# One of the first loads moved to ScalarE's queue, one batch's slots moved behind four value products, and two more clock fillers

## The chip, the cores and the metric

The kernel runs on one core of a Trainium2 chip. The metric is device time of one execution in microseconds, taken as the median of three runs. The engines are called as the profile calls them: PE is TensorE's matrix multiply and PEld its weight load, DVE is VectorE, ACT ScalarE, POOL GpSimd, and SP SyncE, which here issues DMA transfers. The 16 DMA engines of the core carry out what any queue issues.

## The reference

Eight batches of eight heads, 576 positions of 64 numbers, 32 memory slots. A softmax of `phi` over the positions pools `k` and `v` into slots; `q` attends to the slots; the result goes through a gated convolution and two projections.

```python
a = np.exp(phi - phi.max(axis=2)); a = a / (a.sum(axis=2) + 1e-09)
k_m = einsum('bhsm,bhsd->bhmd', a, k);  v_m = einsum('bhsm,bhsd->bhmd', a, v)
scores = q @ k_m.T / sqrt(64);          attn = softmax(scores)
x = (attn @ v_m)                        # heads side by side: 576 x 512 for each batch
gate_pre = sum of conv_w[k] * x shifted by 4 - k positions, k = 0..4
out = (sigmoid(gate_pre) * (x @ w_val)) @ w_out
```

## The kernel before

The program is a list of steps, each a small function of a batch and of a half or a chunk. The string `ORDER` names every step once, and the kernel runs through it from first to last; each step issues its instructions on its engines at that point. So the place of a name in `ORDER` fixes the order of the instructions on every engine, and of the transfers on a DMA queue. An engine takes its instructions strictly in that order. Batches are counted from 0, so the fourth batch has number 3. A star behind a step's name makes it take its other engine.

The steps that matter here:

- `load_top.0.g` brings `phi` of the first batch, group g of four heads, laid out along the positions; `phi_max`, `phi_open` (an exponential on ACT), `phi_turn` (PE transposes) and `phi_place` (a copy, on ACT for group 1 and with a star on DVE for group 0) turn it into the weights `e`.
- `load_kv.0.g.x` brings `k` with a column of ones (x = 1) or `v` (x = 0) of the first batch's group g. `kv_77` is group 0's tile in the listings below, `kv_78` group 1's. All loads are issued by SP.
- `slots.0.g.1` multiplies `e` of group g with its `k` (40 matmul rows of the profile for each g); group 1's last chunk reads `kv_77`. `slots_inv`, `slots_scale` and `slots_turn` divide by the sum and transpose, `slots_place` copies into `kvT`; `scores.0.0` needs `kvT` and the half of `q` that `load_q.0.0` brings.
- `warm.n` is a filler: a product of the identity with n copies of itself, 128 x 128n, which nothing reads. `spread_taps` prepares the convolution's weights on PE.
- In a later batch `slots.b` takes both groups, k and v at once (80 matmul rows of 128x129). `conv.b.s` is the convolution of half s on PE, `value.b.s.t` a quarter of the values' product, which `gated.b.s.y` (DVE) multiplies with the gate two quarters at a time, `project.c` the last projection of a chunk, `mix.b.s` the attention's values.

PSUM has eight banks. `Banks.take` gives a step the banks that were given back longest ago, and a step waits until the one that held them before has read them. DMA completions are counted on eight semaphores that are dealt out in the order of issue.

Of the kernel before, what the change touches and what calls it, by code (L numbers as in the profile page):

```python
# [59 lines left out]
soft_top.0.0 phi_max.1 warm.4 soft_exp.0.0 load_kv.0.1.0 phi_open.1.0 warm.4 spread_taps.0 scores.0.1 place_taps.0  # L60
phi_open.1.1 narrow_sign.o.0 phi_turn.1.0 soft_norm.0.0 narrow_add.o.0 scores_turn.0.1 load_w.v.2 phi_place.1.0
load_w.v.0 soft_top.0.1* load_w.o.1 load_w.v.3 load_rest.1 load_w.p.0 soft_turn.0.0 load_w.o.2 slots.0.0.0 slots.0.1.0
slots_scale.0.0* soft_exp.0.1 phi_turn.1.1 taps.0.0* taps.0.1* wo_high.0* slots_turn.0.0 narrow_round.v.2 load_kv.1.0
conv.0.0 phi_place.1.1 narrow_round.v.0 narrow_size.v.0 soft_high.0.0* narrow_sign.v.0 soft_norm.0.1* slots_place.0.0*
val_rows.0.1 load_kv.1.1 soft_low.0.0 narrow_size.v.2 narrow_add.v.0 soft_turn.0.1 gate.0.0.1 gate.0.0.0 val_rows.0.0
narrow_round.v.3 val_high.0.0* narrow_round.p.0 val_high.0.1* narrow_sign.v.2 narrow_size.v.3 soft_high.0.1*
narrow_sign.v.3 load_top.2 val_low.0.0 conv.0.1 wo_low.0 narrow_size.o.2 value.0.0.0 val_low.0.1 soft_low.0.1
narrow_add.v.2 narrow_add.v.3 value.0.1.0 value.0.0.1 gate.0.1.1 narrow_round.o.2 narrow_sign.p.0 narrow_size.p.0
load_q.1 gate.0.1.0 value.0.1.1 narrow_sign.o.2 narrow_size.o.1 val_rows.0.3 val_rows.0.2 gated.0.0.0 val_high.0.3
val_high.0.2 gated_high.0.0.0 narrow_round.o.1 narrow_sign.o.1 val_low.0.2 val_low.0.3 gated.0.1.0 slots.1 slots_inv.1  # L70
slots_scale.1 value.0.1.2 narrow_add.o.2 phi_max.2 wo_high.2 taps.1.0* gated_low.0.0.0 value.0.0.2 slots_turn.1
value.0.0.3 gated.0.0.1 load_w.o.3 value.0.1.3 gated_high.0.1.0 load_rest.2 narrow_add.o.1 narrow_add.p.0 wo_high.1
gated.0.1.1 wo_low.1 slots_place.1 scores.1.0 wo_low.2 gated_low.0.1.0 scores.1.1 val_rows.1 project.0.0
scores_turn.1.0 project.3.0 phi_spread.2 scores_turn.1.1 narrow_size.o.3 narrow_round.o.3 soft_top.1* narrow_sign.o.3
gated_high.0.0.1 narrow_add.o.3 val_high.1 wo_high.3 project.2.0 load_phi.2 project.1.0 gated_low.0.0.1 soft_exp.1
wo_low.3 load_kv.2.0 val_low.1 gated_high.0.1.1 soft_norm.1* project.0.1 project.1.1 phi_shift.2 soft_turn.1.0
taps.1.1 place.0 gated_low.0.1.1 load_top.3 load_kv.2.1 phi_max.3 soft_turn.1.1 phi_exp.2 mix.1.0 soft_high.1*
scaled.1.0.3.0 scaled.1.0.3.3 tap.1.0.0.0 tap.1.0.1.0 scaled.1.0.2.0 slots.2 tap.1.0.0.4 slots_inv.2 soft_low.1
place.1 scaled.1.0.2.4 tap.1.0.1.2 tap.1.0.0.1 tap.1.0.1.4 slots_scale.2* tap.1.0.0.2 scaled.1.0.3.4 tap.1.0.1.1
# [10 lines left out]
store.1 gated_low.1.1.0* add.2.0.1.1 project.5.1 tap.2.0.0.1 tap.2.0.1.4 scaled.2.0.3.2 scaled.2.0.2.2 place.4  # L90
load_phi.4 load_kv.4.1 add.2.0.1.3 add.2.0.1.2 store.4 tap.2.0.1.2 soft_high.2 soft_low.2 place.5 scores.3.0
tap.2.0.0.3 scores.3.1 val_rows.2 scores_turn.3.0 scores_turn.3.1 mix.2.1 add.2.0.1.4 val_high.2 soft_top.3 load_phi.5
scaled.2.1.2.2 scaled.2.1.3.2 project.6.0 val_low.2 tap.2.1.0.0 scaled.2.1.2.0 tap.2.1.1.0 store.5 phi_max.5
project.7.0 store.2 tap.2.1.1.3 scaled.2.1.2.4 open_gate.2.0.1 tap.2.1.0.3 scaled.2.1.3.1 load_top.6 scaled.2.1.3.4
value.2.0.2 scaled.2.1.3.0 value.2.0.3 scaled.2.1.2.1 add.2.1.1.1 soft_exp.3 tap.2.1.1.2 tap.2.1.0.4 gated.2.0.1
project.6.1 tap.2.1.0.2 project.7.1 add.2.1.1.4 place.6 tap.2.1.0.1 tap.2.1.1.1 value.2.0.0 scaled.2.1.3.3
scaled.2.1.2.3 soft_norm.3 tap.2.1.1.4 value.2.0.1 phi_spread.4 project.8.0 value.2.1.0 project.8.1 gated_high.2.0.1
place.7 open_gate.2.0.0 gated_low.2.0.1 gated.2.0.0 value.2.1.1 gated_high.2.0.0 phi_shift.4* soft_turn.3.0
soft_turn.3.1 open_gate.2.1.0 phi_exp.4 load_q.4 store.6 val_rows.3 add.2.1.1.3 gated_low.2.0.0 soft_high.3
gated.2.1.0 val_high.3 phi_max.6 mix.3.0 tap.3.0.0.0 scaled.3.0.2.0 place.8* scaled.3.0.3.3 slots.4 tap.3.0.1.0  # L100
scaled.3.0.3.0 project.9.0 val_low.3 tap.3.0.0.1 add.2.1.1.2 value.2.1.2 tap.3.0.1.1 tap.3.0.0.4 slots_inv.4
tap.3.0.1.2 scaled.3.0.2.3 add.3.0.1.3 value.2.1.3 scaled.3.0.2.1 scaled.3.0.3.1 scaled.3.0.2.4 gated_high.2.1.0
soft_low.3 open_gate.2.1.1 load_top.7 scaled.3.0.3.4 scaled.3.0.2.2 project.9.1 tap.3.0.0.3 gated.2.1.1 slots_scale.4
scaled.3.0.3.2 tap.3.0.0.2 tap.3.0.1.3 tap.3.0.1.4 mix.3.1 project.10.0 place.9 tap.3.1.1.0 add.3.0.1.4 add.3.0.1.2
tap.3.1.1.1 value.3.0.0 value.3.0.1 tap.3.1.1.3 tap.3.1.1.4 tap.3.1.1.2 tap.3.1.0.0 store.7 open_gate.3.0.0
gated.3.0.0 project.10.1 slots_turn.4 add.3.0.1.1 scaled.3.1.3.0 gated_low.2.1.0 value.3.0.2 scaled.3.1.2.2
gated_high.2.1.1 value.3.0.3 scaled.3.1.2.0 scaled.3.1.3.2 tap.3.1.0.4 scaled.3.1.3.3 scaled.3.1.3.4 place.10
slots_place.4 open_gate.3.0.1 gated_low.2.1.1 tap.3.1.0.1 scores.4.0 add.3.1.1.2 tap.3.1.0.2 tap.3.1.0.3 scores.4.1
gated.3.0.1 val_rows.4 load_kv.5.1 store.9 load_kv.5.0 scores_turn.4.0 load_rest.6 scores_turn.4.1 phi_spread.5
load_q.5 scaled.3.1.2.3 project.12.0 project.11.0 soft_top.4* store.10 gated_high.3.0.0 phi_shift.5 scaled.3.1.3.1  # L110
val_high.4 gated_low.3.0.0 scaled.3.1.2.4 scaled.3.1.2.1 project.11.1 val_low.4 soft_exp.4 soft_norm.4* value.3.1.0
value.3.1.1 project.12.1 add.3.1.1.4 add.3.1.1.3 phi_exp.5 gated_high.3.0.1 open_gate.3.1.0 value.3.1.2 add.3.1.1.1
place.11 place.12 value.3.1.3 soft_turn.4.0 gated.3.1.0 open_gate.3.1.1 mix.4.0 tap.4.0.1.0 tap.4.0.0.0 scaled.4.0.3.1
# [711 lines left out]
```

## Time and profile before

| | us |
|---|---|
| median of three runs (236.61 to 239.53) | 237.48 |
| the profiled execution | 237.75 |
| its span in the profile | 236.0 |
| PE busy | 226.2 |
| DVE, ACT, POOL busy | 185.4, 169.4, 170.2 |

The profiled execution lies 0.27 above the median, and 1.75 of its time lies around the span. PE is busy 96% of the span, so what matters is where it isn't, and which of these gaps other work sets.

### The profile page before, as it was taken

Reading aid. Unit: us, or ns where it says so; the run is one execution under the profiler, and the core shown is the slowest. Engines: PE = TensorE matmul, PEld = TensorE weight load, DVE = VectorE, ACT = ScalarE, POOL = GpSimd, SP = SyncE. Lnnn points to the kernel's source line nnn. Section 1 sums busy time; section 2 is a strip of 40 time slices with the busy share of each in tenths; the row PEclk is TensorE's granted clock in tenths of the full one; section 3 lists DMA queues with packets and bytes.
Section 4 is the critical chain, followed back from the end, with each engine's and each line's share of the span. In section 5 each row is a group of like instructions: output and inputs, shape, how many; then the busy total and the mean of one; then the engine's idle time right before and its main releaser. Section 6 shows DMA issues by size and latency. Waiting matters only on the chain.

```text
span 236.0 us, 6170 instructions
## 1 busy us (share of the span) xinstructions
PE 226.2 (96%) x2496; PEld 175.1 (74%) x2496; DVE 185.4 (79%) x304; ACT 169.4 (72%) x338; POOL 170.2 (72%) x132
## 2 busy tenths in 40 slices
...
GB/s 190 372 413 404 416 410 385 416 207 335 364 138 287 420 287 219 99 274 227 247 157 37 327 375 350 259 0 111 267 7 44 87 49 46 44 92 44 44 64 159
DMA packets 14653, 51.17 MB, mean 217 GB/s; under 512 B 1658, under 2 KB 1954, under 8 KB 11938
## 3 DMA queue, kind: packets, MB, share of 16 engines
...
q8 instruction: 19, 0.31, 0.6%
q14 instruction: 8, 0.07, 0.1%
...
## 4 chain that ended last, share of the span: by engine, by line
PE 90%; DMA 4%; ACT 2%; SPq 1%; issue 1%; POOL 1%
PE banks L727 43%; PE banks L692 22%; PE banks L467 8%; PE banks L626 6%; PE banks L514 4%; DMA q<-in_first_dram 4%; PE banks L593 3%; PE banks L280 1%; PE banks L436 1%; PE banks L498 1%; POOL w_val_sb L381 1%; PE banks L388 1%; ACT o L367 0%; SPq L308 0%; SPq L341 0%
## 5 line engine op out<-in xcount | busy, mean ns | idle before, releaser
L670 POOL TENSOR_TENSOR gate<-gate,x 128x576 f32<-128x576 f32 x49 | 71.7, 1464 | 15.4 <-ACT gate L662 5.3
L727 PE MATMUL banks<-woH,hL 128*128 128x512 f32 x144 | 58.2, 404 | 0.0
L727 PE MATMUL banks<-woH,hH 128*128 128x512 f32 x144 | 56.4, 392 | 0.0
L727 PE MATMUL banks<-woL,hH 128*128 128x512 f32 x144 | 56.3, 391 | 0.0
L662 ACT ACTIVATE x<-banks,cwP 128x288 f32<-128x288 f32 x104 | 48.6, 529 | 5.7 <-PE banks L626 3.7
L653 DVE SCALAR_TENSOR_TENSOR gate<-banks,cwP,gate 128x288 f32<-128x288 f32 x104 | 49.1, 508 | 2.1 <-ACT gate L651 1.2
L267 POOL TENSOR_TENSOR hL<-h,hH 128x576 fp32r<-128x576 f32 (+8 forms) x38 | 38.0, 1019 | 7.8 <-DVE hH L264 4.5
L698 DVE SCALAR_TENSOR_TENSOR h<-gate,banks 128x576 f32<-128x576 f32 x32 | 23.9, 749 | 16.5 <-PE banks L692 12.5
L727 PEld LDWEIGHTS banks<-woH,hL 128*128 128x128 f32 x144 | 27.0, 188 | 9.3 <-issue 2.1
L727 PEld LDWEIGHTS banks<-woH,hH 128*128 128x128 f32 x144 | 27.0, 188 | 6.0
L741 ACT ACTIVATE o<-banks 128x512 f32<-128x512 f32 x26 | 15.7, 603 | 21.1 <-PE banks L727 19.6
L727 PEld LDWEIGHTS banks<-woL,hH 128*128 128x128 f32 x144 | 27.1, 188 | 4.6
L692 PE MATMUL banks<-pL,vwH 128*128 128x288 f32 x128 | 28.6, 305 | 0.0
L692 PE MATMUL banks<-pH,vwH 128*128 128x288 f32 x128 | 27.3, 294 | 0.0
L692 PE MATMUL banks<-pH,vwL 128*128 128x288 f32 x128 | 27.3, 294 | 0.0
L692 PEld LDWEIGHTS banks<-pL,vwH 128*128 128x128 f32 x128 | 21.2, 188 | 6.1 <-issue 3.6
L264 ACT CAST hH<-h 128x576 fp32r<-128x576 f32 (+8 forms) x38 | 18.8, 531 | 7.3 <-DVE h L698 7.3
L267 POOL TENSOR_TENSOR pL<-pT,pH 128x1152 fp32r<-128x1152 f32 (+1 forms) x8 | 19.0, 2372 | 6.4 <-DVE pH L264 6.4
L467 PE MATMUL banks<-kv,e 128*32 128x129 f32 (+2 forms) x656 | 19.3, 263 | 2.8 <-issue 1.4
L675 ACT ACTIVATE gate<-gate 128x576 f32<-128x576 f32 x26 | 18.1, 699 | 4.0 <-DVE gate L653 2.8
L467 PEld LDWEIGHTS banks<-kv,e 128*32 128x32 f32 x656 | 16.3, 128 | 5.7 <-issue 5.3
L692 PEld LDWEIGHTS banks<-pH,vwL 128*128 128x128 f32 x128 | 20.5, 188 | 0.0
...
## 6 DMA issues: line engine op xcount, KB each, us to landing
...
raw<-in_w_val_dram SPq DMA_DIRECT2D x4, 512.0 KB, 10.9
...
```

What stands on the lines that cost most here:

```text
L264: eng.copy(out=out, in_=x) if eng is nc.scalar else eng.tensor_copy(out=out, in_=x)
L267: eng.tensor_tensor(out=out, in0=x, in1=hi.bitcast(F32), op=ALU.subtract)
L467: nc.tensor.matmul(km[j * M:(j + 1) * M, i, n], lhsT=e[:, i, j * M:(j + 1) * M, c], rhs=kvx[c][:, j, :], start=(c == 0), stop=(c == C - 1))
L626: nc.tensor.matmul(live["cv", b, s, g][x * D:(x + 1) * D, t, 0:n], lhsT=weights(g)[rows], rhs=pTs[b % 2][rows, g, s * HALF + i:s * HALF + ...
L653: nc.vector.scalar_tensor_tensor(out=gt, in0=v, scalar=w, in1=gt, op0=ALU.mult, op1=ALU.add)
L662: nc.scalar.activation(out=live[n][:, x], in_=live["cv", b, s, g][:, x, i:i + HALF], func=AF.Identity, scale=cwP[:, 0, i * NP + t:i * NP + ...
L670: eng.tensor_tensor(out=gt, in0=gt, in1=live["x", b, s, g, i], op=ALU.add)
L675: nc.scalar.activation(out=gt, in_=gt, func=AF.Tanh, scale=0.5)
L692: nc.tensor.matmul(vp[:, x, 0:HALF], lhsT=a[:, g, t * P:(t + 1) * P], rhs=p[:, g, s * HALF:(s + 1) * HALF], start=(i == 0), stop=(i == len ...
L698: nc.vector.scalar_tensor_tensor(out=h, in0=live["gate", b, s, y], scalar=1.0, in1=live["vp", b, s, y][:, :, 0:HALF], op0=ALU.add, op1=ALU ...
L727: nc.tensor.matmul(live["proj", c][:, 0], lhsT=ring[a][:, t, at:at + P], rhs=w[:, t], start=(y == 0 and i == 0), stop=(y == 1 and i == len ...
L741: nc.scalar.activation(out=o, in_=x, func=AF.Copy, scale=0.5)
```

## The change

`load_kv.0.1.1`, the `k` of the first batch's group 1, becomes the first step of all, and ACT issues it in place of SP. A `warm.2` stands behind each of the two steps `slots.0.0.1` and `slots.0.1.1`. In the fourth batch `slots.3` and `slots_inv.3` move behind the four steps `value.1.1.2`, `value.1.1.3`, `value.1.0.2` and `value.1.0.3`, with `slots_inv.3` then behind `gated.1.0.1`, and `slots_scale.3*` behind `gated_high.1.1.1`. Nothing else in `ORDER` differs.

```diff
 ORDER = """
-warm.4 warm.4 load_top.0.0 load_w.c.0 load_top.0.1 phi_max.0.0 narrow_size.c.0 phi_open.0.0 phi_max.0.1 phi_open.0.1
...
-load_kv.0.1.1 slots.0.0.1 load_w.v.1 narrow_size.v.1 slots.0.1.1 narrow_add.c.0 load_q.0.0 slots_inv.0.1
...
+load_kv.0.1.1 warm.4 warm.4 load_top.0.0 load_w.c.0 load_top.0.1 phi_max.0.0 narrow_size.c.0 phi_open.0.0 phi_max.0.1
...
+phi_place.0.0* slots.0.0.1 warm.2 load_w.v.1 narrow_size.v.1 slots.0.1.1 warm.2 narrow_add.c.0 load_q.0.0
...
-conv.1.1 slots.3 gate.1.1.1 gated_high.1.0.0 soft_norm.2 value.1.1.2 gate.1.1.0 phi_max.4 slots_inv.3 open_gate.1.0.1
-value.1.1.3 gated.1.1.1 soft_turn.2.0 slots_scale.3* value.1.0.2 load_q.3 value.1.0.3 gated.1.0.1 gated_low.1.0.0
-value.1.1.0 mix.2.0 gated_high.1.1.1 scaled.2.0.2.1 scaled.2.0.2.4 scaled.2.0.3.0 gated_low.1.1.1* value.1.1.1
...
+phi_exp.3 soft_exp.2 add.1.0.1.3 conv.1.1 gate.1.1.1 gated_high.1.0.0 soft_norm.2 value.1.1.2 gate.1.1.0 phi_max.4
+open_gate.1.0.1 value.1.1.3 gated.1.1.1 soft_turn.2.0 value.1.0.2 load_q.3 value.1.0.3 slots.3 gated.1.0.1 slots_inv.3
+gated_low.1.0.0 value.1.1.0 mix.2.0 gated_high.1.1.1 slots_scale.3* scaled.2.0.2.1 scaled.2.0.2.4 scaled.2.0.3.0
...
-        nc.sync.dma_start(out=t, in_=kv[(b - 1) * G + g] if b else piece("vk"[x] + str(g)))
+        rows = kv[(b - 1) * G + g] if b else piece("vk"[x] + str(g))
+        (nc.scalar if (b, g, x) == (0, 1, 1) else nc.sync).dma_start(out=t, in_=rows)
```

The extra line of code moves all line numbers behind it by one in the changed kernel.

On PE at the very start (first batch: fillers, `phi_turn`, `slots`, `spread_taps`, `slots_turn`, `scores`) there stood before:

```order
L422 MATMUL banks<-ident,phT 128x128 x5
L280 MATMUL banks<-ident 128x256
L467 MATMUL banks<-kv_77,e 32x65 x20
L467 MATMUL banks<-kv_78,e 32x65 x16
L467 MATMUL banks<-kv_77,e 32x65 x4
L388 MATMUL banks<-cw_sb,pick_head 128x64 x5
L498 MATMUL banks<-ident,kvd 128x128
L514 MATMUL banks<-q,kvT 32x288 x8
```

and now:

```order
L423 MATMUL banks<-ident,phT 128x128 x5
L280 MATMUL banks<-ident 128x256
L468 MATMUL banks<-kv_77,e 32x65 x20
L280 MATMUL banks<-ident 128x256
L468 MATMUL banks<-kv_78,e 32x65 x16
L468 MATMUL banks<-kv_77,e 32x65 x4
L280 MATMUL banks<-ident 128x256
L389 MATMUL banks<-cw_sb,pick_head 128x64 x5
L499 MATMUL banks<-ident,kvd 128x128
L515 MATMUL banks<-q,kvT 32x288 x8
```

A filler of 128x256 follows each group's products; the order of the rest is kept. On ACT, the first rows of the program (a load of its function table, then the first piece of work on a weight) become

```order
L309 DMA kv_78<-in_first_dram 128x1040
L362 ACT_TABLE_LOAD
L362 ACTIVATE x<-st 40x64
L414 ACTIVATE phT<-phT,top 128x576 x2
L368 ACTIVATE o<-st 40x64
```

where the transfer is the only new row; on SP it is gone from its fifth place, and `w_val`, `q` and `w_out` follow `kv_77` directly. On PE around the fourth batch's slots (behind `conv.1.1`, the row with `taps`) there stood before:

```order
L626 MATMUL banks<-pT_75,taps 64x288 x40
L467 MATMUL banks<-kv_77,e 32x129 x16
L467 MATMUL banks<-rest,e 32x129 x4
L467 MATMUL banks<-kv_78,e 32x129 x16
L467 MATMUL banks<-rest,e 32x129 x4
L692 MATMUL banks<-pL,vwH 128x288 x2
L692 MATMUL banks<-pH,vwL 128x288 x2
L692 MATMUL banks<-pH,vwH 128x288 x2
```

and the end of the same stretch now reads, with four such triples of `value` ahead of it:

```order
L693 MATMUL banks<-pH,vwH 128x288 x2
L468 MATMUL banks<-kv_77,e 32x129 x16
L468 MATMUL banks<-rest,e 32x129 x4
L468 MATMUL banks<-kv_78,e 32x129 x16
L468 MATMUL banks<-rest,e 32x129 x4
L693 MATMUL banks<-pL,vwH 128x288 x2
L693 MATMUL banks<-pH,vwL 128x288 x2
L693 MATMUL banks<-pH,vwH 128x288 x2
L627 MATMUL banks<-pT_73,kvd 64x292 x8
```

The slots now stand one `value` step ahead of `mix.2.0` (the row with `kvd`), instead of directly behind the convolution.

## Rows read from the trace of the kernel before

**Rows 1.** The page: busy time of each engine, share of the span, instructions.

```profile
PE 226.2 (96%) x2496; PEld 175.1 (74%) x2496; DVE 185.4 (79%) x304; ACT 169.4 (72%) x338; POOL 170.2 (72%) x132
```

**Rows 2.** Windows, PE alone: stretch, its length, busy time (rows), granted clock, DMA.

```profile
27.00:64.40 37.40, 37.40 (x641) 1.00 0.92 361
64.46:65.90 1.44, 0.00 (x1) 1.00 0.14 51
67.00:232.40 165.40, 165.40 (x1494) 1.00 0.47 166
```

**Rows 3.** Timeline of the start: start, length, engine, line, what, wait before.

```profile
3.76 0.75 DVE L408 TENSOR_REDUCE top<-phT 128x1 f32<-128x576 f32 x1 [3.76 <-DMA phT<-in_first_dram]
...
5.32 0.75 DVE L408 TENSOR_REDUCE top<-phT 128x1 f32<-128x576 f32 x1 [0.80 <-DMA phT<-in_first_dram]
...
7.62 0.60 PE L280 MATMUL banks<-ident 128*128 128x256 f32 x2
7.83 0.69 ACT L264 COPY e<-banks 128x640 f32<-128x640 f32 x1 [0.63 <-PE banks L422]
...
8.34 0.78 PE L467 MATMUL banks<-kv,e 128*32 128x65 f32 x40
...
9.20 1.04 SPq L308 DMA_DIRECT2D kv<-in_first_dram  x2
...
10.37 0.77 PE L467 MATMUL banks<-kv,e 128*32 128x65 f32 x40 [1.25 <-DMA kv<-in_first_dram]
...
11.07 1.32 PE L388 MATMUL banks<-cw_sb,pick_head 40*128 40x64 f32 x10
...
12.33 0.33 PE L498 MATMUL banks<-ident,kvd 128*128 128x128 f32 x1
12.69 0.29 DVE L264 COPY kvT<-banks 128x128 f32<-128x128 f32 x1 [0.81 <-PE banks L498]
...
13.29 1.22 PE L514 MATMUL banks<-q,kvT 64*32 64x288 f32 x16 [0.64 <-DMA q<-in_first_dram]
...
18.49 0.72 PE L514 MATMUL banks<-q,kvT 64*32 64x288 f32 x16
```

**Rows 4.** Windows of the start: stretch, PE, PEld, DVE, ACT, POOL, clock, DMA share, GB/s.

```profile
1.50:5.30 3.80, 3.76 (x4) 1.15 (x4) 0.75 (x1) 1.53 (x3) 0.00 (x0) 1.00 0.81 245
12.84:16.25 3.41, 2.96 (x18) 1.09 (x19) 1.70 (x4) 2.46 (x5) 1.28 (x1) 0.50 1.04 420
```

**Rows 5.** The four loads of the first batch's k and v, from issue to landing.

```profile
DMA to landing us min/median/max: 6.2/8.7/10.4
```

**Rows 6.** The chain of waits, start: the load of q, the second slots, `val_rows`.

```profile
3.45 9.70 DMA q<-in_first_dram
...
19.99 1.30 PE banks L467 x80
...
26.95 0.45 PE banks L593 x16
```

**Rows 7.** The chain of waits, third batch's slots and around the fourth's.

```profile
51.23 2.37 PE banks L467 x80
...
62.54 1.92 PE banks L467 x61
64.46 1.44 issue
65.90 0.88 PE banks L467 x19
66.78 4.17 PE banks L692 x30
```

**Rows 8.** DMA queues: packets, MB, share; whole span, then only 63.5 to 64.7.

```profile
q8 instruction: 19, 0.31, 0.6%
...
q8 instruction: 1, 0.02, 5.4%
```

**Rows 9.** Timelines of DVE and POOL, 60 to 70.

```profile
62.06 0.75 DVE L698 SCALAR_TENSOR_TENSOR h<-gate,banks 128x576 f32<-128x576 f32 x1
...
65.54 2.13 POOL L559 TENSOR_TENSOR st<-st,ss 128x1152 f32<-128x1152 f32 x1 [1.42 <-DVE ss L558]
```

More of the change, by code (lines that the diff above doesn't have):

```diff
@@ L60 @@
[L60 to L79, printed above, removed]
@@ L90 @@
[L90 to L109, printed above, removed]
@@ L110 @@
[L110 to L113, printed above, removed]
-scaled.4.0.2.3 scaled.4.0.3.0 gated_high.3.1.0* scaled.4.0.2.0 gated.3.1.1 tap.4.0.0.1 phi_spread.6 slots.5
@@ L125 @@
-store.14 phi_spread.7 value.4.0.1 slots.6 value.4.1.0 value.4.1.2 soft_exp.5 phi_shift.7* slots_inv.6 slots_scale.6
-slots_turn.6 phi_exp.7 project.17.0 gated.4.0.0 gated_high.4.0.0 soft_norm.5* open_gate.4.1.0 open_gate.4.1.1
-gated_low.4.0.0 value.4.1.3 value.4.1.1 project.17.1 value.4.0.2 gated.4.1.0 value.4.0.3 slots_place.6 scores.6.0
-gated_high.4.1.0 gated_low.4.1.0 gated.4.1.1 soft_turn.5.0 scores.6.1 place.17 soft_turn.5.1 gated_high.4.1.1
-gated_low.4.1.1 gated.4.0.1 mix.5.0 scores_turn.6.0 gated_high.4.0.1 project.18.0 project.21.0 scaled.5.0.3.2
@@ new lines @@
+slots_inv.0.1 narrow_round.v.1 spread_taps.1 slots_scale.0.1 place_taps.1 load_w.o.0 load_top.1 slots_turn.0.1
+narrow_sign.v.1 narrow_round.o.0 narrow_size.o.0 slots_place.0.1* load_q.0.1 load_kv.0.0.0 scores.0.0 narrow_add.v.1
+scores_turn.0.0 soft_top.0.0 phi_max.1 warm.4 soft_exp.0.0 load_kv.0.1.0 phi_open.1.0 warm.4 spread_taps.0 scores.0.1
+place_taps.0 phi_open.1.1 narrow_sign.o.0 phi_turn.1.0 soft_norm.0.0 narrow_add.o.0 scores_turn.0.1 load_w.v.2
+phi_place.1.0 load_w.v.0 soft_top.0.1* load_w.o.1 load_w.v.3 load_rest.1 load_w.p.0 soft_turn.0.0 load_w.o.2
@@ new lines @@
+slots.0.0.0 slots.0.1.0 slots_scale.0.0* soft_exp.0.1 phi_turn.1.1 taps.0.0* taps.0.1* wo_high.0* slots_turn.0.0
+narrow_round.v.2 load_kv.1.0 conv.0.0 phi_place.1.1 narrow_round.v.0 narrow_size.v.0 soft_high.0.0* narrow_sign.v.0
+soft_norm.0.1* slots_place.0.0* val_rows.0.1 load_kv.1.1 soft_low.0.0 narrow_size.v.2 narrow_add.v.0 soft_turn.0.1
+gate.0.0.1 gate.0.0.0 val_rows.0.0 narrow_round.v.3 val_high.0.0* narrow_round.p.0 val_high.0.1* narrow_sign.v.2
+narrow_size.v.3 soft_high.0.1* narrow_sign.v.3 load_top.2 val_low.0.0 conv.0.1 wo_low.0 narrow_size.o.2 value.0.0.0
@@ new lines @@
+val_low.0.1 soft_low.0.1 narrow_add.v.2 narrow_add.v.3 value.0.1.0 value.0.0.1 gate.0.1.1 narrow_round.o.2
+narrow_sign.p.0 narrow_size.p.0 load_q.1 gate.0.1.0 value.0.1.1 narrow_sign.o.2 narrow_size.o.1 val_rows.0.3
+val_rows.0.2 gated.0.0.0 val_high.0.3 val_high.0.2 gated_high.0.0.0 narrow_round.o.1 narrow_sign.o.1 val_low.0.2
+val_low.0.3 gated.0.1.0 slots.1 slots_inv.1 slots_scale.1 value.0.1.2 narrow_add.o.2 phi_max.2 wo_high.2 taps.1.0*
+gated_low.0.0.0 value.0.0.2 slots_turn.1 value.0.0.3 gated.0.0.1 load_w.o.3 value.0.1.3 gated_high.0.1.0 load_rest.2
@@ new lines @@
+soft_turn.1.1 phi_exp.2 mix.1.0 soft_high.1* scaled.1.0.3.0 scaled.1.0.3.3 tap.1.0.0.0 tap.1.0.1.0 scaled.1.0.2.0
+slots.2 tap.1.0.0.4 slots_inv.2 soft_low.1 place.1 scaled.1.0.2.4 tap.1.0.1.2 tap.1.0.0.1 tap.1.0.1.4 slots_scale.2*
+tap.1.0.0.2 scaled.1.0.3.4 tap.1.0.1.1 project.2.1 scaled.1.0.2.3 slots_turn.2 load_phi.3 load_q.2 scaled.1.0.2.2
+tap.1.0.0.3 phi_spread.3 project.3.1 place.2 add.1.0.1.4 store.0 slots_place.2 phi_shift.3 scores.2.0 load_kv.3.0
+tap.1.0.1.3 place.3 scaled.1.0.2.1 load_rest.3 scaled.1.0.3.1 scores.2.1 value.1.0.0 scaled.1.0.3.2 scores_turn.2.0
@@ new lines @@
+gated.1.1.0 load_rest.5 project.4.0 soft_turn.2.1 tap.2.0.1.3 tap.2.0.0.0 store.3 scaled.2.0.2.3 slots_place.3*
+tap.2.0.0.4 gated_low.1.0.1 tap.2.0.1.1 scaled.2.0.3.3 gated_high.1.1.0 scaled.2.0.3.4 load_rest.4 project.4.1
+load_top.5 tap.2.0.0.2 load_kv.4.0 store.1 gated_low.1.1.0* add.2.0.1.1 project.5.1 tap.2.0.0.1 tap.2.0.1.4
+scaled.2.0.3.2 scaled.2.0.2.2 place.4 load_phi.4 load_kv.4.1 add.2.0.1.3 add.2.0.1.2 store.4 tap.2.0.1.2 soft_high.2
+soft_low.2 place.5 scores.3.0 tap.2.0.0.3 scores.3.1 val_rows.2 scores_turn.3.0 scores_turn.3.1 mix.2.1 add.2.0.1.4
@@ new lines @@
+project.8.1 gated_high.2.0.1 place.7 open_gate.2.0.0 gated_low.2.0.1 gated.2.0.0 value.2.1.1 gated_high.2.0.0
+phi_shift.4* soft_turn.3.0 soft_turn.3.1 open_gate.2.1.0 phi_exp.4 load_q.4 store.6 val_rows.3 add.2.1.1.3
+gated_low.2.0.0 soft_high.3 gated.2.1.0 val_high.3 phi_max.6 mix.3.0 tap.3.0.0.0 scaled.3.0.2.0 place.8*
+scaled.3.0.3.3 slots.4 tap.3.0.1.0 scaled.3.0.3.0 project.9.0 val_low.3 tap.3.0.0.1 add.2.1.1.2 value.2.1.2
+tap.3.0.1.1 tap.3.0.0.4 slots_inv.4 tap.3.0.1.2 scaled.3.0.2.3 add.3.0.1.3 value.2.1.3 scaled.3.0.2.1 scaled.3.0.3.1
@@ new lines @@
+scaled.3.0.2.4 gated_high.2.1.0 soft_low.3 open_gate.2.1.1 load_top.7 scaled.3.0.3.4 scaled.3.0.2.2 project.9.1
+tap.3.0.0.3 gated.2.1.1 slots_scale.4 scaled.3.0.3.2 tap.3.0.0.2 tap.3.0.1.3 tap.3.0.1.4 mix.3.1 project.10.0 place.9
+tap.3.1.1.0 add.3.0.1.4 add.3.0.1.2 tap.3.1.1.1 value.3.0.0 value.3.0.1 tap.3.1.1.3 tap.3.1.1.4 tap.3.1.1.2
+tap.3.1.0.0 store.7 open_gate.3.0.0 gated.3.0.0 project.10.1 slots_turn.4 add.3.0.1.1 scaled.3.1.3.0 gated_low.2.1.0
+value.3.0.2 scaled.3.1.2.2 gated_high.2.1.1 value.3.0.3 scaled.3.1.2.0 scaled.3.1.3.2 tap.3.1.0.4 scaled.3.1.3.3
@@ new lines @@
+value.3.1.2 add.3.1.1.1 place.11 place.12 value.3.1.3 soft_turn.4.0 gated.3.1.0 open_gate.3.1.1 mix.4.0 tap.4.0.1.0
+tap.4.0.0.0 scaled.4.0.3.1 scaled.4.0.2.3 scaled.4.0.3.0 gated_high.3.1.0* scaled.4.0.2.0 gated.3.1.1 tap.4.0.0.1
+phi_spread.6 slots.5 gated_low.3.0.1 scaled.4.0.3.3 store.11 load_phi.6 scaled.4.0.2.2 gated_high.3.1.1*
+scaled.4.0.3.2 project.13.0 tap.4.0.1.1 scaled.4.0.2.1 tap.4.0.0.4 soft_turn.4.1 tap.4.0.0.3 add.4.0.1.3
+scaled.4.0.2.4 gated_low.3.1.0 tap.4.0.1.2 tap.4.0.1.4 tap.4.0.0.2 scaled.4.0.3.4 project.13.1 gated_low.3.1.1
@@ new lines @@
+load_kv.6.1 scores.5.0 place.16 open_gate.4.0.0 scores_turn.5.0 scaled.4.1.3.4 scores.5.1 add.4.1.1.3 add.4.1.1.1
+val_rows.5 scores_turn.5.1 value.4.0.0 scaled.4.1.3.2 scaled.4.1.2.2 store.15 val_high.5 load_q.6 soft_top.5 val_low.5
+add.4.1.1.2 add.4.1.1.4 store.14 phi_spread.7 value.4.0.1 slots.6 value.4.1.0 value.4.1.2 soft_exp.5 phi_shift.7*
+slots_inv.6 slots_scale.6 slots_turn.6 phi_exp.7 project.17.0 gated.4.0.0 gated_high.4.0.0 soft_norm.5*
+open_gate.4.1.0 open_gate.4.1.1 gated_low.4.0.0 value.4.1.3 value.4.1.1 project.17.1 value.4.0.2 gated.4.1.0
@@ new lines @@
+value.4.0.3 slots_place.6 scores.6.0 gated_high.4.1.0 gated_low.4.1.0 gated.4.1.1 soft_turn.5.0 scores.6.1 place.17
+soft_turn.5.1 gated_high.4.1.1 gated_low.4.1.1 gated.4.0.1 mix.5.0 scores_turn.6.0 gated_high.4.0.1 project.18.0
+project.21.0 scaled.5.0.3.2 tap.5.0.0.0 gated_low.4.0.1 load_kv.7.0 scaled.5.0.3.0 tap.5.0.1.0 scaled.5.0.2.2 store.16
+scores_turn.6.1 load_kv.7.1 project.18.1 soft_top.6 scaled.5.0.2.0 scaled.5.0.3.1 soft_high.5 add.5.0.1.2
+scaled.5.0.2.1 project.21.1 tap.5.0.1.4 add.5.0.1.1 tap.5.0.0.1 tap.5.0.1.3 tap.5.0.1.1 tap.5.0.1.2 tap.5.0.0.3
```

116 lines of the change are left out of this document (58 added, 58 removed).

## The prediction

> **What bounds the kernel.** I read the page first: PE is busy 96% of the span, the others at most 79% [rows 1]. So the question is where PE's few idle microseconds lie. Windows of PE answer it [rows 2]: from 27.0 to 64.4 and again from 67.0 to 232.4 it is busy all the time, at a granted clock of 1.00 (2.4 GHz). Behind 27 there is one gap, 1.44 us at 64.46. The rest of the idle time lies before 27, at the start. The end therefore moves by as much as `val_rows` at 26.95 [rows 6] moves, and by what becomes of the gap. The third view is the timeline of the start [rows 3], the fourth the chain of waits around the gap [rows 7].
>
> **The gap at 64.46.** The chain shows the fourth batch's slots as 61 matmul rows, 1.44 us of "issue" (a wait for nothing that the profile names), then the last 19 [rows 7]. It lies in the middle of `kv_78`'s products, where no load and no bank is awaited. Exactly there, between 63.5 and 64.7, one of the 19 packets of the queue that carries instructions runs [rows 8]: 0.31 MB in 19 packets is 16 KB each. My reading is that PE had used up its code and waited for the next piece. `conv.1.1` and `slots.3` stand one behind the other, and both are many short instructions, so PE runs through its code faster here than elsewhere. The Trainium skill ("Runtime: NRT & Kernel Launch", section "Instruction fetch mechanics") says that the engine fetches the next 16 KiB of code while it runs the current one, and that crossing a boundary is mostly hidden. The windows show no second gap behind 27, though most of the other 18 packets run there, which agrees; at this one the trace differs. If the Trainium skill's rule held here too, the gap would have another cause and might stay; that is a rival below.
>
> Now the four `value` steps come in between. The 30 `value` rows behind the gap take 4.17 us [rows 7], so four steps of six rows take 24 x 0.139 = 3.3 us, and the code behind the boundary is wanted that much later than in the trace, where it was late by 1.44. So the gap should go. What is late next? Three things:
> - `value.1.1.2` needs the two banks that `gated.1.0.0` reads. DVE does that at 62.06 and is done at 62.81 [rows 9]; before, the slots covered it. The convolution ends at 62.54, so this costs about 0.3.
> - `mix.2.0` needs `soft_turn.2.0` and `gated.1.0.1`. POOL is done with the softmax at 67.67 [rows 9]; DVE then transposes and does `gated.1.0.1`, each an operation of the size of the 0.75 in [rows 9]: 69.2. PE comes there at 62.85 + 3.3 + 2.37 (a full `slots`, [rows 7]) + 0.8 for `value.1.1.0` = 69.3. So between 0 and 0.2.
> - SP issues later those loads that wait until `slots.3` has read its tiles, and the loads behind them; the batch they belong to comes tens of microseconds later, so nothing.
>
> The stretch from 62.54 to the end of four `value` steps is now 4.24 + 3.3 = 7.5 us. It becomes 0.3 + 3.3 + 2.37 = 6.0. That is 1.5, less 0.1 for the second point: the gain is **1.4 us**, between 0 (the gap stays and the wait for DVE is hidden in it) and 1.5. DVE's `slots_inv.3` moves behind two `gated`, ACT's `slots_scale.3` behind a cast; the transposes that they feed come a `mix` and a `value` later on PE, some 1.5 us, and both are short, so I cost this at nothing; without that cover it would be tenths.
>
> **The load on ACT's queue.** Before, PE had the first group's slots done at 9.12 and waited 1.25 for `kv_78` [rows 3]. That wait goes if the load lands by then, which it should: on SP it was the fifth transfer, now it is the first of its own queue. ACT's issue costs it about 0.5, as SP's two at 9.20 took 1.04 [rows 3], and its table load moves back by that; its first work comes at 3.7 us, so that is free. But the 520 KB take DMA time from `phi`, whose two halves DVE awaits at 3.76 and 5.32 [rows 3]. At the 420 GB/s that the queues reach later [rows 4] they are 1.3 us. The lower bound of the delay is 0: from 1.5 to 5.3 the DMA engines were busy to 0.81 only and moved 245 GB/s [rows 4], so a second queue may fill what was free. That is 0.19 x 3.8 = 0.7 us of the 1.3. The upper bound is 1.3 for each half. I take +1.0 for the first half, which begins side by side with the new load, and +0.7 for the second. The Trainium skill ("DMA: Bandwidth & Descriptors", section "Rules for kernel authors") speaks against the change here: transfers issued by several engines run on the same 16 DMA engines and interleave, so spreading them gives no bandwidth. By it the delay is the upper bound for both halves.
>
> With +0.7, the second half's maximum starts at 6.0. In the trace `phi_place` of group 1 (ACT) ends 3.2 us after that start, at 8.52 [rows 3]; now at 9.2. The filler ahead of the slots ends 0.7 later too, at 8.9. First slots 8.9 to 9.7, filler, second slots 10.1 to 10.9, against 11.14: 0.25 won.
>
> **The fillers.** A `warm.2` is two rows of 128x256 that take 0.60 with the drain [rows 3], about 0.4 in a row of work. The first is in the times just given. The second lies on the path too: `slots_turn` at 12.33 came right behind `spread_taps` [rows 3], which now begins 0.4 later. So `slots_turn` is at 12.33 - 0.25 + 0.4 = 12.5 and `kvT` done at 13.15. `q` lands at 3.45 + 9.70 = 13.15 [rows 6], and its place in the sum of bytes is the same. So `scores.0.0` stays at 13.3, and neither the early load nor the fillers move it by themselves.
>
> What the fillers may change is the clock. From 12.84 to 16.25 it was granted at 0.50, 1.2 GHz [rows 4], after a stretch in which PE had waited 1.25 and 0.64 us and had mostly done products of 32 columns of weights. There `scores.0.0` took 1.22, where the second half takes 0.72 at full clock [rows 3]: 0.5 on the path from `scores.0.0` through DVE and POOL to ACT's exponential, and ACT and DVE work without a pause from there to `val_rows`. With the waits gone and 0.8 us of full-width work added, I take it that the clock stays up: 0.5. It isn't all kept. The `v` of group 1, the later of the two loads at 9.2, lands 10.4 after its issue at 9.8, at 20.1 [rows 3, 5]; its half of the slots began at 19.99 + 0.65 = 20.64 [rows 6] and can come at most 0.45 sooner. So the start gives **0.4 us**, between -0.6 (loss; all of phi's delay, clock as before) and +0.7 (no delay of phi, and all loads a little sooner).
>
> **The sum.** 1.4 + 0.4 = 1.8. Against the profiled execution, 237.75, that is 235.95. This execution was 0.27 above the median of 237.48, so I expect the median at **235.7**; its own bounds, with 1.2 to 2.2 won, are 235.3 to 236.3.
>
> **The rivals.**
> 1. `phi` is late by the upper bound. Both halves come 1.3 later, first slots at 9.5, `slots_turn` at 13.1, `scores.0.0` at 13.9, and the clock falls as before: the start loses 0.6, and 0.8 of the 1.4 remains: 236.7. For it speaks that the DMA engines were busy to 0.81 even in the slow first microseconds; against it, that the idle share is real. The Trainium skill's rule on several queues, above, gives this time.
> 2. The change doesn't do what it says at the gap: the 1.44 have another cause, or move with the code to the next stretch of short instructions. Then only the start counts: 237.1. Against it speaks the packet [rows 8].
> 3. Slower: the clock stays down from the beginning. With phi's first half late, PE idles from 5.3 to 6.4, ahead of its first transposes, where before it went straight on. If the clock rises only behind that work, the path from `phi_turn` to `slots_turn` runs at 1.2 GHz: transposes 0.9, two slots 1.6, two fillers 0.8, `spread_taps` 1.3, each up to twice as long. That is 4.6 more at most, of which the 1.25 and 0.64 that PE waited before hide 1.9: 2.7 on `scores.0.0`. With the 1.4 kept, that is 1.3 slower: 238.8. It decides from a granted clock below 1.00 between 6 and 10 us.
>
> **Chances.** Forecast 0.50, rival 1 0.22, rival 2 0.15, rival 3 0.07; 0.06 for what I don't see, on both sides. The range of 8 in 10 takes the forecast with its bounds, the first two rivals, and the half a microsecond that medians of three runs spread over 2.9 may be off: 234.6 to 237.4. A change of 2%, 4.75 us, is about what a measurement of this kernel can tell from none. No case reaches it: faster 0.03, within 0.94, slower 0.03.
>
> **What would show it.** Right: no "issue" wait of PE within the fourth batch's slots; `value.1.1.2` starting about 0.3 behind the convolution; `mix.2.0` some 1.8 earlier than at 66.78 + 4.17 = 70.95 [rows 7]; no wait for `kv` between the first two slots; DVE's first maximum near 4.8; a clock of 1.00 from 12.8 to 16.3; `val_rows` near 26.5. Wrong: an instruction packet with a gap of PE in another place, or PE waits behind 67, where there were none, which would mean that another engine or a load can't follow a PE that is 1.8 ahead.

## The result, and the profile after

The changed kernel takes 240.31 us (median of 20 runs, 238.25 to 242.26), the one before beside it 237.55 (20 runs). The ratio is 1.0096, with an interval of 1.0074 to 1.0118: 2.3 us slower, where 1.8 faster was forecast. Of the first profiled executions, that of the changed kernel (241.84) was among its slowest and that of `fill_only`, below, took 371.38; neither is shown. The one shown here is a second of the changed kernel, of 239.64 with a span of 237.9, one of twelve more runs that gave 1.0079 (1.0052 to 1.0106).

Windows of PE alone in the changed kernel (stretch, its length, busy time and rows, granted clock, DMA share, GB/s); they answer to [rows 2]:

```profile
28.70:63.70 35.00, 35.00 (x564) 1.00 0.91 357
64.50:79.00 14.50, 14.50 (x185) 1.00 0.62 202
79.45:81.23 1.78, 0.00 (x0) 1.00 1.06 437
82.30:233.00 150.70, 150.70 (x1367) 1.00 0.44 155
```

The gap in the fourth batch's slots is gone. In its place stands a new one of 1.8 us, some 15 us later, while the DMA engines move 437 GB/s. That is one loss. The other is in the start, here as rows of the timeline of PE up to `val_rows.0.0`, with DVE's maxima of `phi` among them; they answer to [rows 3]:

```profile
1.48 3.78 PE L280 MATMUL banks<-ident 128*128 128x512 f32 x4 [1.48 <-POOL ident masks.py:199]
...
5.13 1.61 DVE L409 TENSOR_REDUCE top<-phT 128x1 f32<-128x576 f32 x2 [5.13 <-DMA phT<-in_first_dram]
...
6.75 1.34 PE L423 MATMUL banks<-ident,phT 128*128 128x128 f32 x5 [1.49 <-ACT phT L414]
7.89 1.06 PE L280 MATMUL banks<-ident 128*128 128x256 f32 x2
8.74 1.27 PE L423 MATMUL banks<-ident,phT 128*128 128x128 f32 x5
9.81 0.64 PE L280 MATMUL banks<-ident 128*128 128x256 f32 x2
10.37 0.78 PE L468 MATMUL banks<-kv,e 128*32 128x65 f32 x40
11.08 0.70 PE L280 MATMUL banks<-ident 128*128 128x256 f32 x2
11.71 0.77 PE L468 MATMUL banks<-kv,e 128*32 128x65 f32 x40
...
15.09 0.72 PE L515 MATMUL banks<-q,kvT 64*32 64x288 f32 x16 [0.46 <-DVE kvT L264]
...
28.20 0.45 PE L594 MATMUL banks<-w_val_sb,kvT 64*32 64x128 f32 x16 [0.28 <-POOL w_val_sb L382]
```

Read the durations of like work. The filler of two rows takes 1.06 at 7.89 and 0.64 at 9.81, and the first transposes 1.34: PE works at 1.2 GHz up to about 9.8, where in the trace before the same filler took 0.60 at 7.62 [rows 3]. The trace's record of the granted clock agrees: it begins only at 9.88, with 1.00. Ahead of the first transposes PE had stood idle from 5.26 to 6.75, waiting for `phi`. Between the first slots and the scores lie 4.72 us. `scores.0.0` is at 15.09 against 13.29, `val_rows.0.0` at 28.20 against 26.95 [rows 6]: +1.25.

The chain of waits that ends in the new gap (start, length, what):

```profile
71.96 0.66 SPq L309
72.62 0.04 issue
72.67 7.83 DMA out_dram<-o
...
80.58 0.61 ACT o L742
81.19 0.04 issue
81.23 1.09 PE banks L594 x16
```

and SP's timeline in the same stretch:

```profile
69.98 0.33 SPq L318 DMA_DIRECT2D rest<-in_kv_rest_dram  x1
70.36 0.42 SPq L748 DMA_DIRECT2D out_dram<-o  x1
70.84 0.42 SPq L318 DMA_DIRECT2D kv<-in_kv_rest_dram  x1
71.37 0.55 SPq L290 DMA_DIRECT2D phT<-in_phi_t_dram  x1
71.96 0.66 SPq L309 DMA_DIRECT2D kv<-in_kv_dram  x1
72.67 0.44 SPq L748 DMA_DIRECT2D out_dram<-o  x1
```

`val_rows.2` needs the banks that `place.5` empties; `place.5` (ACT, L742) needs an `o` tile, which `store.1` has to have written out first; `store.1` (SP, 72.67) stands behind loads of a later batch, and the first of these, `load_rest.5` (69.98), waits for `slots.3` to have read its tile. With `slots.3` done 3.2 later (the load behind it was issued at 66.81 before), the store lands at 80.50, and `place.5` waits 1.95 for it (ACT's timeline at 80.58). Before, `store.1` was issued at 70.36 and took 8.2 to land, at 78.6, just as ACT came to `place.5`:

```profile
78.67 0.60 ACT L741 ACTIVATE o<-banks 128x512 f32<-128x512 f32 x1
```

The three terms add up: +1.25 at the start, -1.44 + 0.31 at the old gap, +1.80 at the new one, together +1.92; the spans differ by 237.9 - 236.0 = 1.9.

### The profile page after: what moved, and what is told of

It is laid out like the page before. It is cut to its first block, busy times and chain, and to the rows that moved or that the text cites. A ratio compares the mean times of both kernels' runs of the same rounds, so it can differ in the third digit from the quotient of the medians.

```text
span 240.1 us, 6180 instructions
## 1 busy us (share of the span) xinstructions
PE 228.3 (95%) x2500; PEld 176.6 (74%) x2500; DVE 185.6 (77%) x304; ACT 169.1 (70%) x338; POOL 170.3 (71%) x132
## 4 chain that ended last, share of the span: by engine, by line
PE 81%; DVE 6%; DMA 5%; ACT 3%; POOL 2%; issue 1%; SPq 0%; DVEq 0%; ACTq 0%; POOLq 0%
PE banks L728 40%; PE banks L693 19%; PE banks L468 7%; PE banks L627 4%; DMA out_dram<-o 3%; PE banks L594 3%; PE banks L515 3%; DMA phT<-in_first_dram 2%; PE banks L280 1%; DVE st L522 1%; PE banks L423 1%; POOL st L560 1%; DVE banks L557 1%; DVE banks L540 1%; DVE st L541 1%
## 5 line engine op out<-in xcount | busy, mean ns | idle before, releaser
L742 ACT ACTIVATE o<-banks 128x512 f32<-128x512 f32 x26 | 15.7, 604 | 23.2 <-PE banks L728 19.4
L693 PEld LDWEIGHTS banks<-pH,vwH 128*128 128x128 f32 x128 | 20.4, 188 | 0.0
```

Of the source, the lines that this page charges most:

```text
L693: nc.tensor.matmul(vp[:, x, 0:HALF], lhsT=a[:, g, t * P:(t + 1) * P], rhs=p[:, g, s * HALF:(s + 1) * HALF], start=(i == 0), stop=(i == len ...
L742: nc.scalar.activation(out=o, in_=x, func=AF.Copy, scale=0.5)
```

## The experiments

Each was timed beside the kernel before, and the differences in us are the ratio less one, times its median. Theory A: the early load starves `phi`, and the slots' move makes a store late. Theory B: the fillers are to blame. Theory C: only the start is. D and E came later.

**One part at a time.** `load_only`: the load on ACT's queue, first of all.

```diff
+load_kv.0.1.1 warm.4 warm.4 load_top.0.0 ...
-phi_place.0.0* load_kv.0.1.1 slots.0.0.1
+        (nc.scalar if (b, g, x) == (0, 1, 1) else nc.sync).dma_start(out=t, in_=rows)
```

> Only the load of k on ScalarE's queue, first of all; no fillers, fourth batch's slots as before. Theory A (the load starves phi, and PE then works at 1.2 GHz up to about 13): slower by 1.5 to 3, DVE's first maximum at 5.5 as in the changed kernel, scores.0.0 at 16 or later, and the 1.44 gap still there. Theory B (the two fillers hold the start up, the load is innocent): between 0.3 faster and 0.5 slower, scores.0.0 near 13.3 to 14. Theory C (the whole loss is the start, the slots' move is a gain of 1.3 by itself): slower by some 4.

`fill_only`: the two fillers.

```diff
-slots.0.0.1 load_w.v.1 narrow_size.v.1 slots.0.1.1
+slots.0.0.1 warm.2 load_w.v.1 narrow_size.v.1 slots.0.1.1 warm.2
```

> Only the two fillers, one behind each of the first two slots; k on SyncE's queue, fourth batch's slots as before. Theory A: within 0.4 of before, since the first filler lies in the wait for k (1.25) and the second costs 0.4 or gives back 0.5 by the clock. Theory B: slower by 1 to 3, as most of the loss is theirs.

`slots_only`: the fourth batch's order as in the changed kernel.

```diff
-conv.1.1 slots.3 gate.1.1.1 gated_high.1.0.0 soft_norm.2 value.1.1.2 ... value.1.0.3 gated.1.0.1
+conv.1.1 gate.1.1.1 gated_high.1.0.0 soft_norm.2 value.1.1.2 ... value.1.0.3 slots.3 gated.1.0.1
```

> Only the fourth batch's slots behind the four value products; start as before. Theory A (the gap of 1.44 goes, but store.1 stands on SyncE behind loads that wait for these slots, so place.5 gets its buffer 2.2 late and val_rows.2 with it): slower by 0.8 to 1.4, val_rows.2 waits 2 us for place.5 and place.5 for a store. Theory C (that wait is there only because the start was late): faster by 1.0 to 1.4, no wait at val_rows.2.

`slots_stores`: the same, and two stores moved on SP.

```diff
+store.3 store.1 load_rest.5
-store.3
-store.1
```

> As slots_only, and store.3 and store.1 stand on SyncE ahead of load_rest.5, so that they don't wait for the slots. Theory A: the wait at val_rows.2 is gone and the gap too: faster by 1.0 to 1.4. If the gain of the gap is lost elsewhere (a load that is now late, DVE behind): within 0.4 of before, with another wait of PE behind 67. Theory C: as slots_only.

| | ratio to before | interval | us |
|---|---|---|---|
| `load_only` | 0.9984 | 0.9950 to 1.0018 | -0.4 |
| `fill_only` | 0.9950 | 0.9923 to 0.9976 | -1.2 |
| `slots_only` | 1.0038 | 1.0005 to 1.0070 | +0.9 |
| `slots_stores` | 0.9936 | 0.9908 to 0.9965 | -1.5 |

Two parts do no harm alone, and one does, though its interval only just clears 1. Theory B falls as it stands: the fillers alone are a gain, and more of one than theory A's 0.4. The mean granted clock points to where it comes from: it is 0.993 or less in 21 of the 31 runs of the kernel before beside them, and in one of the fillers' own eleven (without the one of 371.38). There is no trace of them alone to read. Theory C falls too: with the start as before, `slots_only` has the same wait. Its timeline of PE, then that of `slots_stores`, of SP and ACT:

```profile
80.19 1.09 PE L593 MATMUL banks<-w_val_sb,kvT 64*32 64x512 f32 x16 [1.47 <-ACT o L741]
```

```profile
58.55 0.93 SPq L747 DMA_DIRECT2D out_dram<-o  x2
68.60 0.34 SPq L317 DMA_DIRECT2D rest<-in_kv_rest_dram  x1
...
77.14 0.60 ACT L741 ACTIVATE o<-banks 128x512 f32<-128x512 f32 x1
```

With both stores at 58.55, ten microseconds ahead of the first load that waits, `place.5` follows ACT's cast without a wait, and PE has no gap behind 27 but the 0.3 for DVE. The stores' place is worth 0.9 + 1.5 = 2.4 us by the runs. The two traces, with spans of 236.7 and 234.6, show 1.47 of it at the wait and 0.53 in their starts (`val_rows.0.0` at 27.33 and 26.80), though the program is the same there; so part of the 2.4 may not be the stores'. Theory A holds at the slots, but not at the start, where it asked 1.5 to 3 from the load alone.

`load_only` had a surprise. Its profiled execution, one of its five shortest (235.88):

```profile
6.79 0.85 PE L423 MATMUL banks<-ident,phT 128*128 128x128 f32 x5 [1.52 <-ACT phT L414]
7.48 0.60 PE L280 MATMUL banks<-ident 128*128 128x256 f32 x2
...
9.02 1.34 PE L468 MATMUL banks<-kv,e 128*32 128x65 f32 x80
...
12.25 0.72 PE L515 MATMUL banks<-q,kvT 64*32 64x288 f32 x16 [0.38 <-DVE kvT L264]
...
25.48 0.45 PE L594 MATMUL banks<-w_val_sb,kvT 64*32 64x128 f32 x16 [0.31 <-POOL w_val_sb L382]
```

`phi` is as late as in the changed kernel (PE waits up to 6.79), but here the clock is up at 6.79 already (0.85 and 0.60; its record begins at 5.53), and `scores.0.0` comes at 12.25, a whole microsecond earlier than before, since `q` no longer ends that wait. `val_rows.0.0` is at 25.48, 1.47 earlier than before. But its runs lie in two groups, five at 235.6 to 236.2 and seven at 237.0 to 239.1. So theory D: what the early load does depends on whether the clock comes up in spite of PE's idle time at 5.3 to 6.8. Theory E: the parts add up, and the slots' move costs more behind an early load.

**Load and fillers together, and a longer filler.** `load_fill` is `load_only` with the two fillers; `load_warm` is `load_only` with

```diff
-warm.4 warm.4 load_top.0.0
+warm.4 warm.4 warm.4 load_top.0.0
```

`fill_slots_stores` is `slots_stores` with the two fillers, `after_warm_stores` the changed kernel with the third `warm.4` and the stores moved.

> The load on ScalarE's queue and the two fillers, fourth batch's slots as before. Theory D (the two don't add: with the load PE idles from 5.3 to 7 ahead of its first transposes and in most runs works at 1.2 GHz up to about 13; there a filler takes 1.1 and two of them lie on the path): slower by 0.8 to 2, first slots at 1.3 and fillers at 1.1 in its profile. Theory E (the two add up as alone, and the changed kernel lost because the slots' move costs more behind an early load): faster by 1 to 1.6.

> The load on ScalarE's queue and one warm.4 more at the very start (four rows of 128x512 in three steps' place, 1.9 more of PE's work), no warm.2 behind the slots, fourth batch's slots as before. Theory D: PE no longer idles from 5.3 to 7, its clock is up by 8.5 in every run, first slots take 0.8: faster by 0.8 to 1.5, with the slow half of the runs of load_only gone. If phi's lateness itself is the cost, whatever the clock: as load_only, 0.4 faster, or up to 0.3 worse where the filler ends behind phi's arrival.

> The two fillers, the slots behind the four value products, store.3 and store.1 ahead of load_rest.5; k stays on SyncE's queue. If the parts add (1.2 and 1.5 alone): faster by 2.2 to 3.0, no wait of PE from 27 to 232 but the 0.3 for DVE, clock up throughout the start. If an earlier start brings the store or another load back into the way: faster by 1.5 or less, with a wait of PE behind 67.

> The changed kernel with one warm.4 more at the very start and with store.3 and store.1 ahead of load_rest.5. Theory D: both losses are mended (2.4 by the stores, 1.5 to 3 by the clock): faster than before by 2 to 3. If only the stores' wait is mended: within 0.5 of before.

| | ratio to before | interval | us |
|---|---|---|---|
| `load_fill` | 0.9982 | 0.9951 to 1.0013 | -0.4 |
| `load_warm` | 0.9941 | 0.9909 to 0.9973 | -1.4 |
| `fill_slots_stores` | 0.9919 | 0.9886 to 0.9951 | -1.9 |
| `after_warm_stores` | 0.9953 | 0.9928 to 0.9977 | -1.1 |

`load_warm` bears out theory D. Its timeline of PE:

```profile
1.48 5.08 PE L280 MATMUL banks<-ident 128*128 128x512 f32 x6 [1.48 <-POOL ident masks.py:199]
6.64 0.86 PE L423 MATMUL banks<-ident,phT 128*128 128x128 f32 x5
7.34 0.60 PE L280 MATMUL banks<-ident 128*128 128x256 f32 x2
...
8.88 1.34 PE L468 MATMUL banks<-kv,e 128*32 128x65 f32 x80
...
12.12 0.72 PE L515 MATMUL banks<-q,kvT 64*32 64x288 f32 x16 [0.38 <-DVE kvT L264]
```

PE works through to `phi`'s arrival, the clock is up at 6.64, and the runs lie between 236.1 and 237.7: the longer group of `load_only` is gone. All three profiles with the third `warm.4` show the 0.86 and 0.60; of the five with the early load and without it, four show 1.34 and 1.06, and only `load_only` doesn't. The records of the clock say the same: they begin at 9.67 to 13.30 in those four, at 5.53 in `load_only`, and at 4.61 to 7.25 in the eight others. That the longer runs of `load_only` are those with the late clock isn't shown, as none of them has a trace.

The trace of `load_warm` shows one thing more. `val_rows.0.0` is 1.38 earlier than before (25.57), but the span is only 0.4 shorter. The gap in the slots is 1.56, and `val_rows.2` takes 1.99 at 78.01 where it took 1.15, for `place.5` waits for its store although the slots weren't moved:

```profile
78.26 0.60 ACT L742 ACTIVATE o<-banks 128x512 f32<-128x512 f32 x1 [0.85 <-DMA out_dram<-o]
```

In `load_only` it waits 0.37. So the store takes back a part of what an earlier start wins, too.

`load_fill`'s rows at the start are those of the changed kernel, and two more follow:

```profile
6.87 1.34 PE L423 MATMUL banks<-ident,phT 128*128 128x128 f32 x5 [1.61 <-ACT phT L414]
8.00 1.06 PE L280 MATMUL banks<-ident 128*128 128x256 f32 x2
...
10.33 0.77 PE L468 MATMUL banks<-kv,e 128*32 128x65 f32 x40
...
15.04 0.72 PE L515 MATMUL banks<-q,kvT 64*32 64x288 f32 x16 [0.46 <-DVE kvT L264]
...
65.75 0.68 PE L468 MATMUL banks<-kv,e 128*32 128x129 f32 x16 [0.28 <-issue]
...
142.69 1.33 PE L468 MATMUL banks<-kv,e 128*32 128x129 f32 x40 [0.50 <-DMA kv<-in_kv_dram]
```

From here the start can be sized. First slots at 10.33 against 9.02: the late clock costs 1.2 once the 0.08 between the transposes' starts is taken off. From first slots to scores 4.71 against 3.23: two fillers cost 1.5 on the path, 0.75 each. Against `load_only`'s -1.47 that makes +1.2, as measured (28.16 against 26.95 in `load_fill`). So in this company the fillers, a gain alone, are the larger loss of the start. Without the early load they cost nothing there (`val_rows.0.0` at 26.89 in `fill_slots_stores`): before, PE waits 1.25 for `kv` and 0.64 for `q` [rows 3], and the early load takes these waits away.

The miss is `load_fill`'s time. With `val_rows.0.0` 1.2 later it should have been about 1.2 slower, as theory D said, and its runs are as fast as before. In its trace the gap in the fourth batch's slots is 0.28 where it had been 1.44, which takes 1.16 back, and PE waits 0.50 for a load of `kv` at 142.69, where the trace before has no wait: +0.55 in all, and its span is 0.7 longer. So the smaller gap explains most of the miss; why the runs show nothing of the rest is open. Theory E's 1 to 1.6 faster didn't come either. But E has a point: in this company the slots' move has almost no gap left to win (0.28 against the 0.31 for DVE). `after_warm_stores` is 1 us short of what I expected, for I had left the fillers' 1.5 in it out. `fill_slots_stores` is a miss as well: 1.9 where the parts together asked 2.2 to 3.0, with no wait of PE behind 27 but the 0.3 for DVE; where the rest went isn't found.

**The changed kernel mended.** `after_again` is the changed kernel; `after_stores` has only the two stores moved; `load_warm_slots_stores` is `after_warm_stores` without the two fillers; `late_slots_stores` is `slots_stores` with the load on ACT's queue, but later:

```diff
-phi_open.0.0 phi_max.0.1 ... phi_place.0.0* load_kv.0.1.1
+phi_open.0.0 load_kv.0.1.1 phi_max.0.1 ... phi_place.0.0*
```

> The changed kernel once more, beside the next ones. Theory D: slower by 1.5 to 3 as before, with a clock that comes up at 9 or later, and PE waiting 2 us at val_rows.2 for place.5, which waits for store.1.

> The changed kernel, and only store.3 and store.1 moved ahead of load_rest.5 on SyncE. If the wait of 2.2 at val_rows.2 is all of what the slots' move costs: 2.0 to 2.5 faster than the changed kernel on the same chip, so between 0.5 slower and 0.5 faster than before. If the wait only hides another loss: within 1 of the changed kernel, with a PE wait elsewhere behind 60.

> After_warm_stores without the two fillers behind the slots. If each of these fillers lies on the path with its 0.7: faster than before by 2.3 to 3.3, scores.0.0 at 12.2 and val_rows.0.0 at 25.6. If later loads bind there (q, the v of group 1) whatever PE does: as after_warm_stores, 1.1 faster.

> No fillers, no warm.4 more; slots and stores moved; k of the second group on ScalarE's queue, but behind phi_open of the first group, so that it is issued at about 5.3, when both halves of phi have landed or nearly. Theory D: phi lands at 3.7 and 5.3 as before, k by 8.5, no wait between the first slots, clock up at 5 to 7: faster by 2.3 to 3.3. If k comes too late so (9 or later): as slots_stores, 1.5 faster.

| | ratio to before | interval | us |
|---|---|---|---|
| `after_again` | 1.0079 | 1.0052 to 1.0106 | +1.9 |
| `after_stores` | 1.0006 | 0.9980 to 1.0032 | +0.1 |
| `load_warm_slots_stores` | 0.9920 | 0.9895 to 0.9946 | -1.9 |
| `late_slots_stores` | 1.0157 | 1.0129 to 1.0184 | +3.7 |

Moving two stores takes 1.7 off the changed kernel (1.0079 less 1.0006, times 237.55), about the 1.80 of the wait in its trace. What is left of the gain at the gap (1.1) is used up by the start: `val_rows.0.0` is at 28.34 in `after_stores`, 1.39 later than before.

`load_warm_slots_stores` joins what the traces show to pay: the early load, a filler that keeps PE busy until `phi` is there, the slots' move, the stores ahead. Windows of its PE:

```profile
25.90:61.00 35.10, 35.10 (x564) 1.00 0.95 375
61.85:228.00 166.15, 166.15 (x1567) 1.00 0.48 167
```

Its profile starts `val_rows.0.0` at 25.43 and has no gap behind it but 0.31; its median of 235.75 stands against 237.55. I had expected 2.3 to 3.3, and 1.9 came; its profiled execution (235.02) was its shortest. `fill_slots_stores`, without the early load, measures the same 1.9, and `slots_stores`, with neither, 1.5, with intervals that overlap. So the traces show an earlier start with the early load (`val_rows.0.0` at 25.43 and 26.89, spans of 233.2 and 234.6), but the runs don't show that it is worth more than the fillers.

`late_slots_stores`, 3.7 slower where 1.5 to 3.3 faster was expected, refutes that an issue on a second queue can come when it is convenient. Its timelines of ACT and PE:

```profile
4.46 0.38 ACTq L309 DMA_DIRECT2D kv<-in_first_dram  x1
```

```profile
8.97 0.77 PE L468 MATMUL banks<-kv,e 128*32 128x65 f32 x40 [1.13 <-DMA kv<-in_first_dram]
12.78 1.31 PE L468 MATMUL banks<-kv,e 128*32 128x65 f32 x40 [3.04 <-DMA kv<-in_first_dram]
```

Issued at 4.46, with an empty queue of its own, the load is awaited up to 12.78, 8.3 us later, so the slots wait 3.0 for it. SP had issued seven loads before it, and it came no earlier than if it had been issued behind most of these: it lands at 12.65, and `q`, the sixth on SP, at 12.8. From 4.5 to 8.1 the view of the DMA queues has no packet of ACT's queue, and all 144 of them run from 8.1 to 12.3; in `load_only`, issued at 0.74, they run from 2.0 to 5.0. What holds them back isn't shown. An idle queue of its own doesn't put a transfer ahead here. In the wait the clock falls, too: it is granted at 0.50 from 11.56 to 21.80, and `val_rows.0.0` is at 31.65, 4.7 later than before.

## Why the prediction was wrong

- **The gap.** Right. The "issue" gap is gone in all nine traces with the slots moved, and stands in the three other experiments whose traces are used here. The reading as code agrees, though no run tests it by itself: an instruction packet runs just ahead of each of the four gaps, and PE goes on 1.25 to 1.5 us behind its end (64.64 and 65.90 before, 62.54 and 63.79 in `load_only`, 64.26 and 65.75 in `load_fill`, 63.22 and 64.64 in `load_warm`). Rival 2 is refuted. `value.1.1.2` waits 0.31 for DVE, as forecast (0.3), and `mix.2.0` doesn't wait (0 to 0.2 forecast). What wasn't foreseen is that the gap's size isn't fixed: 0.28, 0.79, 1.44 and 1.56 in four programs that differ only in the start.
- **"SP issues later those loads ... so nothing."** This is the step that failed most. The loads themselves could wait; but I looked at who needs them and not at what is queued behind them on SP. There stands `store.1`, and `place.5` needs its tile with no time to spare: before, it ran at 78.67, right behind a cast, and the store had landed at 78.6. Cost 1.8 in the trace, 1.7 and 2.4 by the two pairs with the stores moved. The forecast said itself what a PE wait behind 67 would mean, and none of its rivals had it.
- **phi's delay.** Forecast +1.0 and +0.7. DVE's first maximum starts at 5.13 against 3.76, +1.4, above the upper bound of 1.3. It does both halves in one go and ends at 6.74, where before the second ended at 5.32 + 0.75: +0.7, as forecast. Rival 1 wanted 1.3 for both. The Trainium skill's rule there ("DMA: Bandwidth & Descriptors", "Rules for kernel authors") has it that several queues interleave and add no bandwidth. The first half agrees: beside the new load `phi` comes 1.4 later. But where the engines weren't full the second queue did add: from 1.50 to 5.30, 300 GB/s in the changed kernel and 301 in `load_only` against 245 [rows 4]. The window of `load_only`, in the columns of [rows 4]:

```profile
1.50:5.30 3.80, 3.77 (x4) 1.16 (x4) 0.13 (x1) 0.95 (x1) 0.00 (x0) 1.00 0.95 301
```

- **"Its place in the sum of bytes is the same" (q at 13.15).** Wrong, in the kernel's favour: `q` lands 8.2 us after its issue in the changed kernel and 7.8 in `load_only`, where it took 9.70 [rows 6], `scores.0.0` doesn't wait for `q` in any trace with the early load, and runs at 12.25 in `load_only`. With the clock up the load alone is worth 1.47 at `val_rows.0.0`, where I had 0.4 for load, fillers and clock together.
- **"I take it that the clock stays up."** Once up, it does: `scores.0.0` takes 0.72 in the trace above and not 1.22 [rows 3]. But it doesn't come up in time. That was rival 3, with a chance of 0.07: PE idle ahead of the first transposes, the path from there at 1.2 GHz. Its price was 2.7 on `scores.0.0`; the trace above shows 1.8, and the first one of the changed kernel 3.6. I had weighed it by phi's delay, as one case; but PE's idle time was in the sum of my own forecast already (DVE's maximum at 4.8 instead of 3.76), and nothing in the rows said how much of it the clock would bear.
- **The fillers.** 0.4 each on the path, 0.75 measured. I had taken the rows' rate from a stretch of work; here one takes 0.63 from its start to the next step's (11.08 to 11.71), and the slots that it parts no longer overlap (0.77 twice, where both together took 1.34).

The sum, by the trace above: start +1.25 where -0.4 was forecast, gap -1.13 where -1.4 was, and +1.80 where there was nothing. The start's +1.25 is, by the traces of `load_only` and `load_fill`, about -1.5 for the load, +1.2 for the late clock and +1.5 for the two fillers.

Open: why the gap has four sizes, and what sets the moment at which the clock comes up. It differs between executions whose start is the same: its record begins at 6.01 before, at 7.25 in `slots_only` and at 6.73 in `slots_stores`. In `load_only` it begins at 5.53, just behind the end of the first fillers at 5.26, so almost none of PE's idle time lies ahead of it.
